# A routed mixture of experts behind attention: router folded into the weights, experts sorted by size

## The chip, the core and the metric

One core of a Trainium2 chip runs the whole program in one launch. The time is device microseconds from the first to the last instruction with what the launch adds around them, the median of several executions. Engines are named as in the profile: PE (TensorE products), PEld (its weight loads), DVE (VectorE), ACT (ScalarE), POOL (GpSimd), SP (SyncE, which here only issues DMAs).

## What is computed

Attention over 2 x 8 heads of 576 tokens, a gated feed-forward, and a mixture of eight experts in which every token goes to one expert and an expert takes at most 288 tokens.

```python
x = block_causal_attention(q, k, v)               # -> 1152 tokens x 512
x = (x @ w_a * (x @ w_b)) @ w_out                 # 512 -> 1536 -> 512, weights in float64
logits = x @ w_gate                               # 512 -> 8
expert = argmax(logits); gate = softmax(logits)[expert]
# token i is kept if fewer than 288 earlier tokens chose its expert
h = maximum(x @ w1[expert], 0)                    # 512 -> 1024
out[i] = gate * (h @ w2[expert])                  # 1024 -> 512; 0 where not kept
```

## The kernel before

Float32 accuracy is reached with pairs: a tensor is split into a first part in the fast product format (`fp32r`) and the rest in the same format, and a product takes three products of parts (first with first, first with second, second with first). ACT makes the first part with a cast, DVE or POOL the second with a subtraction. Where a plain float32 product is used (the logits), no split is needed.

**First feed-forward** (after the attention; lines 426 and 503 to 504). For each of twelve groups of 128 columns and each of three chunks of 384 tokens, `prod` (L426) forms two products of 12 steps each, and `gate_mul` multiplies them into `g_sb` (ACT copies one, DVE multiplies). The weights come as float64 words; `bits64` (L371 to L383) turns a tile into float32 with one ACT step and four DVE steps. Tiles called raw and bits have two buffers each, used in turn by the groups of `w_a`, `w_b` and by `w_out` (`load_wout`, `bits_wout`, `split_wout`), which is made ready in the same loop.

**Second product and router.** For each tile of 128 tokens t, `g_split` (L478, L479) splits g, `y_part` (L622) runs 12 x 3 products of 512 columns, `y_row` (L629) copies the result to a row buffer. Between the products of tile t stand the router's steps of tile t - 1: `y_turn` (L636) turns the row, `logits` (L644) multiplies it by `w_gate` in plain float32, `choose` (L651 to L665) finds the expert, `place` (L674 to L692) counts tokens with a triangular product, and POOL scatters the row into `xdisp`, a buffer in DRAM with 288 slots for each expert. All of that is in program order on each engine.

**Experts.** In the order of their numbers, two steps overlapped: the first product of expert e (`one`), then the second of expert e - 1 (`two`). Chunks of 1 MB of `w1` and `w2` are fetched by SP in a fixed order through five buffers (L573) and split by ACT (L591) and by DVE or POOL (L594), whatever the expert's size. `xload` (L775 to L779) reads the expert's rows, `x_turn` (L805, L813) turns them. An expert with over 64 tokens takes the wide way: products of 288 (or 256) columns at L841, then blocks of 128 tokens at L927 and a last block of 32 with both parts side by side (`stacked`, L823). One with 1 to 64 tokens has both parts of its 64 rows side by side in the stationary operand (L823), sums them (`both`, L973 and L974), turns the result (`turn_few`, L890) and multiplies again. Every choice is a branch (`tc.If`, L867 and others) on all engines, on a count read into registers. `put` (L909) scatters the result to `out` from POOL.

Of the kernel before, what the change touches and what calls it, by code (L numbers as in the profile page):

```python
# [27 lines left out]
NC_IDENT, NC_TRI, NC_IOTA, NC_TOK = 0, 128, 256, 264  # L28
# [29 lines left out]
def const_columns(n_tok, n_exp):  # L58
    """Identity, strict upper triangle, expert numbers, token numbers with two zeros after each."""
    import numpy as np  # L60

    nt = n_tok // P
    c = np.zeros((P, NC_TOK + 3 * nt), np.float32)
    c[:, NC_IDENT:NC_IDENT + P] = np.eye(P)
    c[:, NC_TRI:NC_TRI + P] = np.triu(np.ones((P, P)), 1)
    c[:, NC_IOTA:NC_IOTA + n_exp] = np.arange(n_exp)
    c[:, NC_TOK::3] = np.arange(P)[:, None] + P * np.arange(nt)[None, :]
    return c
# [3 lines left out]
def fused_kernel(ctx: ExitStack, tc, q, k, v, w_a, w_b, w_out, w_gate, w1, w2, consts, out, cap):  # L72
# [27 lines left out]
    ident = cst[:, NC_IDENT:NC_IDENT + P]  # L100
    xdisp = dpool.tile([NSLOT, ROW], F32, name="xdisp")
# [7 lines left out]
    # ------------------------------------------------------------ attention  # L109
# [8 lines left out]
    # rows of the dispatch buffer that no token fills: zeros, and a token number out of range  # L118
# [311 lines left out]
    def ahead(f, j):  # L430
        """Products of the first tokens, while the last heads are still turned."""
# [26 lines left out]
    # ------------------------------------------------ first feed-forward, a * b  # L458
# [5 lines left out]
    wg_sb = gp.tile([P, KD, E], F32, name="wg_sb")  # L464
    nc.sync.dma_start(out=wg_sb, in_=w_gate.rearrange("(k p) e -> p k e", p=P))
# [34 lines left out]

    def gate_mul(f, c, pa, pb):
# [9 lines left out]
    load_wout(0)  # L511
    es_y = ExitStack()
    psY = es_y.enter_context(tc.tile_pool(name="psY", bufs=2, space=PSUM))
    with tc.tile_pool(name="psF", bufs=3, space=PSUM) as psF:
        for f in range(NF):
            for c in range(NCH):
# [26 lines left out]
    es_r = ExitStack()  # L543
    wr_pool = es_r.enter_context(tc.tile_pool(name="wr_pool", bufs=5, side="right"))
    wq_pool = es_r.enter_context(tc.tile_pool(name="wq_pool", bufs=2, side="right"))
    HALF = 512
    NSL = 6
    CPE = F2 // HALF
    KC = KF2 // KD
    PER = CPE + KC  # L550
    chunks = [(0, 0, c) for c in range(CPE)]
    for e in range(E):
        if e + 1 < E:
            chunks += [(e + 1, 0, c) for c in range(CPE)]
        chunks += [(e, 1, c) for c in range(KC)]
    place_of = {x: n for n, x in enumerate(chunks)}
    wc = {}
    wpools = [wq_pool]
    state = {"raw": 0, "split": 0}
    raws = {}  # L560

    def fetch_chunk():
        n = state["raw"]
        if n >= len(chunks):
            return
        state["raw"] += 1
        e, which, c = chunks[n]
        raw = wr_pool.tile([P, KD, HALF], F32, tag="wraw", name=f"wraw{n}")
        if which == 0:
            src = w1[e, :, c * HALF:(c + 1) * HALF].rearrange("(k p) f -> p k f", p=P)  # L570
        else:
            src = w2[e, c * KD * P:(c + 1) * KD * P, :].rearrange("(k p) f -> p k f", p=P)
        nc.sync.dma_start(out=raw, in_=src)  # L573
        raws[n] = raw

    def split_next():
        """Pieces of the split of the next chunk into its two parts."""
        n = state["split"]
        if n >= len(chunks):
            return []  # L580
        state["split"] += 1
        while state["raw"] <= n:
            fetch_chunk()
        pool = wpools[0] if n % NSL < 2 else wpools[1]
        raw = raws.pop(n)
        hi = pool.tile([P, KD, HALF], F32R, tag="whi", name=f"whi{n}")
        lo = pool.tile([P, KD, HALF], F32R, tag="wlo", name=f"wlo{n}")
        wc[chunks[n]] = (hi, lo)

        def piece(a):  # L590
            nc.scalar.copy(hi[:, a:a + 2], raw[:, a:a + 2])  # L591
            e, which, c = chunks[n]
# [448 lines left out]
```

## Time and profile before

| | us |
|---|---|
| median of 3 runs (lowest, highest) | 554.28 (553.45, 555.82) |
| span of the profiled execution | 551.1 |
| PE busy, share of the span | 494.1, 90% |
| DVE | 333.3, 60% |
| ACT | 259.9, 47% |
| POOL | 212.8, 39% |
| mean granted clock of PE | 0.965 |

The profiled execution is one of its own; its span leaves out the launch. A busy PE is not PE at its peak, since products are pipelined: start to start is the pace, and the duration of one product is longer than its pace. Times in the trace are microseconds from the start of the span. The reader should look at stretches, not at the shares of the whole span: attention ends at about 140 us, the first feed-forward at 283.5, the second product at 378, and the experts fill the rest.

### The profile page before, as it was taken

How to read it: one execution, taken by the hardware profiler on the slowest of the kernel's cores; microseconds unless marked ns; L12 is line 12 of the kernel's file. 1: busy time of each engine (PE TensorE's matmuls, PEld its weight loads, DVE VectorE, ACT ScalarE, POOL GpSimd, SP SyncE). 2: the span in 40 equal slices, each digit the busy share in tenths (PEclk: the TensorE clock that was granted, in tenths of full speed). 3: DMA queues.
4: the chain of work that ended last, by engine and by line, in shares of the span. 5: the costliest groups of instructions: out<-in, count | busy, mean ns of one | idle time of the engine just before them, and what ended most of it. 6: DMA issues, size and time to landing. Idle time of an engine off the chain costs nothing. (4 is left out here: it accounts for less than half of the span.)

```text
span 551.1 us, 8356 instructions
## 1 busy us (share of the span) xinstructions
PE 494.1 (90%) x2860; PEld 437.7 (79%) x2860; DVE 333.3 (60%) x567; ACT 259.9 (47%) x502; POOL 212.8 (39%) x215
## 2 busy tenths in 40 slices
PE   5899989999999999999999999995397989897764
PEld 4799879999999999999997766773297888575553
DVE  4799899863565566763333445333578535257991
ACT  4798687863242343322222423211566545357740
POOL 6557584770041522313100301011324606184971
PEclk9899999999999999999999999998589999999887
DMA  6774575100544442421027122000479736475810
GB/s 149 204 242 124 124 230 177 29 2 1 180 143 140 150 153 78 152 81 74 1 94 288 40 96 96 19 24 2 157 251 296 262 141 201 162 259 179 271 52 4
DMA packets 67251, 73.39 MB, mean 133 GB/s; under 512 B 31394, under 2 KB 43810, under 8 KB 67184
## 3 DMA queue, kind: packets, MB, share of 16 engines
q1 hardware_dynamic: 65584, 69.09, 39.2%
q0 software_dynamic: 1456, 3.29, 1.6%
q8 instruction: 38, 0.62, 0.5%
q14 instruction: 29, 0.24, 0.1%
q10 hardware_dynamic: 144, 0.15, 0.1%
HBM read 62.12 MB, written 11.72 MB: 134 GB/s over the span
## 5 line engine op out<-in xcount | busy, mean ns | idle before, releaser
L426 PE MATMUL p<-xTh,hi 128*128 128x384 f32 x272 | 91.1, 335 | 1.6 <-ACT asb L503 0.8
L426 PE MATMUL p<-xTh,lo 128*128 128x384 f32 x272 | 90.9, 334 | 0.0
L426 PE MATMUL p<-xTl,hi 128*128 128x384 f32 x272 | 90.9, 334 | 0.0
L594 DVE TENSOR_TENSOR wlo<-wraw,whi 128x1024 fp32r<-128x1024 f32 x43 | 78.3, 1837 | 14.4 <-ACT whi L591 13.5
L594 POOL TENSOR_TENSOR wlo<-wraw,whi 128x1024 fp32r<-128x1024 f32 x21 | 57.4, 2747 | 44.9 <-ACT whi L591 29.4
L314 POOL TENSOR_TENSOR PB<-PB,rs 128x64 f32<-128x64 f32 (+8 forms) x72 | 54.0, 782 | 32.3 <-DVE rs L307 18.8
L591 ACT CAST whi<-wraw 128x1024 fp32r<-128x1024 f32 x64 | 63.9, 1047 | 4.5 <-issue 3.3
L426 PEld LDWEIGHTS p<-xTh,hi 128*128 128x128 f32 x272 | 51.0, 188 | 2.2 <-ACT asb L503 1.2
L389 POOL TENSOR_TENSOR wol<-wob,woh 128x1024 fp32r<-128x1024 f32 x6 | 14.4, 2401 | 96.9 <-ACT woh L388 96.9
L426 PEld LDWEIGHTS p<-xTl,hi 128*128 128x128 f32 x272 | 51.1, 188 | 0.0
L426 PEld LDWEIGHTS p<-xTh,lo 128*128 128x128 f32 x272 | 51.0, 188 | 0.0
L622 PE MATMUL py<-woh,gh 128*128 128x512 f32 x108 | 45.7, 423 | 0.0
L841 PE MATMUL ph<-xt,whi 128*128 128x288 f32 (+1 forms) x192 | 40.2, 307 | 5.8 <-ACTq L887 1.7
L692 POOL DMA_INDIRECT xdisp<-row,sl x9 | 9.0, 999 | 88.8 <-ACT row L629 83.9
L622 PE MATMUL py<-woh,gl 128*128 128x512 f32 x108 | 42.8, 396 | 0.0
L622 PE MATMUL py<-wol,gh 128*128 128x512 f32 x108 | 42.5, 394 | 0.0
L296 ACT ACTIVATE PB<-sc,nm 128x64 f32<-128x64 f32 (+8 forms) x72 | 37.7, 534 | 6.7 <-DVE nm L286 6.4
L330 DVE TENSOR_TENSOR PTl<-pT,PTh 128x512 fp32r<-128x512 f32 (+1 forms) x56 | 33.4, 623 | 8.2 <-ACT PTh L326 7.9
L841 PEld LDWEIGHTS ph<-xt,whi 128*128 128x128 f32 x192 | 32.0, 199 | 7.0 <-ACTq L887 2.1
L504 DVE TENSOR_TENSOR g_sb<-asb,p 128x384 f32<-128x384 f32 x34 | 18.4, 552 | 31.6 <-PE p L426 17.7
L416 POOL TENSOR_TENSOR lo<-bits,hi 128x1024 fp32r<-128x1024 f32 x12 | 28.8, 2396 | 20.2 <-ACT hi L410 20.2
L286 DVE TENSOR_REDUCE nm<-sc 128x1 f32<-128x64 f32 (+8 forms) x72 | 32.1, 478 | 6.8 <-PE sc L266 6.6
(147 smaller groups left out, 1153.4 us busy)
## 6 DMA issues: line engine op xcount, KB each, us to landing
wraw<-in_moe_w SPq DMA_DIRECT2D x32, 1024.0 KB, 6.4
raw<-in_moe_w_a SPq DMA_DIRECT2D x12, 512.0 KB, 3.6
raw<-in_moe_w_b SPq DMA_DIRECT2D x12, 512.0 KB, 4.7
wor<-in_moe_w_out SPq DMA_DIRECT2D x6, 1024.0 KB, 4.9
xdisp<-zrow SPq DMA_DIRECT2D x6, 774.0 KB, 5.4
out<-zrow SPq DMA_DIRECT2D x3, 768.0 KB, 4.8
qkv<-in_q SPq DMA_DIRECT2D x16, 128.0 KB, 2.5
qkv<-in_k SPq DMA_DIRECT2D x16, 128.0 KB, 2.8
```

The costliest lines, as they stand in the source:

```text
L286: nc.vector.tensor_reduce(out=soft[n][0][:, col[i]:col[i] + 1], in_=view, op=ALU.max, axis=ax, negate=True)
L296: nc.scalar.activation(out=dst, in_=view, func=AF.Exp, bias=nm[:, col[i]:col[i] + 1], accum_out=sm[:, col[i]:col[i] + 1],)
L314: nc.gpsimd.tensor_tensor(out=x, in0=x, in1=r, op=ALU.mult)
L330: nc.vector.tensor_tensor(out=PTl[:, sl], in0=src, in1=f32(PTh[:, sl]), op=ALU.subtract)
L389: nc.gpsimd.tensor_tensor(out=lo, in0=f32(m), in1=f32(hi), op=ALU.subtract)
L416: nc.gpsimd.tensor_tensor(out=lo, in0=f32(m), in1=f32(hi), op=ALU.subtract)
L426: nc.tensor.matmul(ps, lhsT=lt, rhs=rt, start=(n_ == 0), stop=(n_ == len(seq) - 1))
L504: nc.vector.tensor_tensor(out=g_sb[:, f, c * CH:(c + 1) * CH], in0=asb, in1=pb, op=ALU.mult)
L591: nc.scalar.copy(hi[:, a:a + 2], raw[:, a:a + 2])
L594: eng.tensor_tensor(out=lo[:, a:a + 2], in0=raw[:, a:a + 2], in1=f32(hi[:, a:a + 2]), op=ALU.subtract)
L622: nc.tensor.matmul(s["py"], lhsT=lt[:, f], rhs=rt[:, f], start=(f == 0 and i == 0), stop=(f == NF - 1 and i == 2))
L841: nc.tensor.matmul(ph[:, 0:n].rearrange("p (g c) -> p g c", c=G), lhsT=lt, rhs=rt, start=(n_ == 0), stop=(n_ == len(seq) - 1),)
```

## The change

- **Router ahead of the second product.** Since `logits = g @ w_out @ w_gate`, the product `w_out @ w_gate` is formed once. For that `w_out` comes a second time, transposed on the host (`in_w_outT`, 6 MB in float64), through the same raw and bits buffers. `gate_rows` multiplies a tile by `w_gate` padded to 32 columns in plain float32, the four row blocks to four groups of 32 PSUM partitions; `gate_cols` adds the four and turns them with one product against `sel`, a 0/1 matrix. The logits of all tokens are then formed from `g_sb` in one go (`logit_rows`), `choose` and `place` run once for all tiles, while the first tile of the second product runs. Each tile's row is scattered right after `y_row`.
- **Experts sorted.** `place` ranks the experts by count; slots in `xdisp` go by rank. Rank, expert's number and the number of experts with over 32 tokens are read into registers. SP fetches weights by a register's expert number, eight chunks already during the second product, into a ring of ten buffers.
- **One tree of branches.** `arms` picks one of nine straight programs, `experts(n)`, for n large experts. In it each large expert has 288 columns, blocks of 128 (the later ones only if its count asks for them) and a tail of 32; for the split all second parts are on DVE.
- **Small experts in float32.** Experts with at most 32 tokens go in groups of four, 32 rows each, unsplit. `few1` forms the four row blocks of a contraction in four groups of 32 PSUM partitions; `few_turn` adds and turns them with `sel`; `few2` does the second product likewise, `few_sum` adds its four groups into the expert's place, `group_out` scales and writes all four at once. `line` interleaves these steps of four experts by hand. Experts without tokens are not fetched.

```diff
+    def gate_rows(c):
+        m = wt_bits.pop(c)
+        pw = psW.tile([P, 2 * P], F32, tag="pw", name=f"pw{c}")
+        for kd in range(KD):
+            nc.tensor.matmul(pw[G * kd:G * (kd + 1)], lhsT=wgp[:, kd], rhs=f32(m)[:, kd], start=True, stop=True)
+        t = xpool.tile([P, 2 * P], F32, tag="wpT", name=f"wpT{c}", bufs=2)
+        nc.scalar.copy(t, pw)
+        wt_bits[c] = t
+    def gate_cols(c):
+        t = wt_bits.pop(c)
+        pf = psW.tile([P, 2, G], F32, tag="pf", name=f"pf{c}")
+        for i in range(2):
+            nc.tensor.matmul(pf[:, i], lhsT=t[:, i * P:(i + 1) * P], rhs=sel[:, 0:G], start=True, stop=True)
+        nc.scalar.copy(Wp[:, 2 * c:2 * c + 2], pf)
...
                 if c == 1 and f % 2 == 0:
+                    bits_wot(f // 2)
+                    load_wout(f // 2)
+                if c == 1 and f % 2:
                     bits_wout(f // 2)
                     if f // 2 + 1 < NWO:
-                        load_wout(f // 2 + 1)
+                        load_wot(f // 2 + 1)
                     split_wout(f // 2)
+                    gate_cols(f // 2)
+                if c == 0 and f % 2:
+                    gate_rows(f // 2)
...
+    def logit_rows(c):
+        pl = psG.tile([P, CH], F32, tag="pl", name=f"pl{c}", bufs=3)
+        for f in range(NF):
+            j = f % KD
+            nc.tensor.matmul(
+                pl[G * j:G * (j + 1)], lhsT=Wp[:, f], rhs=g_sb[:, f, c * CH:(c + 1) * CH],
+                start=(f < KD), stop=(f >= NF - KD), skip_group_check=True,
+            )
+        nc.scalar.copy(lgp[:, c], pl)
...
+    def choose():
+        for t in range(NT):
+            nc.tensor.matmul(plg[:, t], lhsT=flat[:, t * P:(t + 1) * P], rhs=sel[:, 0:E], start=True, stop=True)
...
+    def place():
+        nc.tensor.matmul(pp, lhsT=tri, rhs=oh, start=True, stop=False)
+        for t in range(NT):
+            nc.tensor.matmul(pp[:, t + 1:], lhsT=ones, rhs=bc(oh[:, t], 1, NT - t), start=False, stop=(t == NT - 1))
...
+    for c in range(NCH):
+        logit_rows(c)
     for t in range(NT):
-        y_part(t, 0, 2)
-        if t > 0:
-            y_turn(t - 1)
+        y_part(t, 0, 4)
+        if t == 0:
+            choose()
         if t + 1 < NT:
             g_split(t + 1)
-        if t > 0:
-            y_part(t, 2, 5)
-            logits(t - 1)
-            y_part(t, 5, 8)
-            choose(t - 1)
-            y_part(t, 8, 11)
-            place(t - 1)
-            y_part(t, 11, NF)
...
+        y_part(t, 4, NF)
         y_row(t)
-        if t in (2, 4):
-            split_to(t // 2)
-    y_turn(NT - 1)
-    logits(NT - 1)
-    choose(NT - 1)
-    place(NT - 1)
+        if t == 0:
+            place()
+            numbers_sp()
+            for r in range(2):
+                for c in range(NCK):
+                    raws[r, c] = ring[r * NCK + c]
+                    fetch(r, c)
+        if t == 5:
+            numbers()
+        scatter(t)
...
+    def few1(a, i):
+        hp = new("hp", [P, CPE, HALF], bufs=2, pool="few")
+        for c in range(CPE):
+            ph = psH.tile([P, HALF], F32, tag="ph", name=f"pf{a}_{i}_{c}_{uid[0]}")
+            for kd in range(KD):
+                nc.tensor.matmul(
+                    ph[kd * G:(kd + 1) * G], lhsT=g["xt"][:, kd, i * G:(i + 1) * G], rhs=raws[a + i, c][:, kd],
+                    start=True, stop=True,
+                )
+            (nc.vector.tensor_copy if c else nc.scalar.copy)(hp[:, c], ph)
+    def few_turn(a, i):
+        for f in range(KF2):
+            nc.tensor.matmul(pt[:, f], lhsT=hp[:, f * P:(f + 1) * P], rhs=sel[:, 0:G], start=True, stop=True)
+        g[i] = new("hg", [P, KF2, G], bufs=2, pool="few")
+        nc.scalar.activation(out=g[i], in_=pt, func=AF.Relu)
+    def few2(a, i):
+        for f in range(KF2):
+            j = f % KD
+            nc.tensor.matmul(
+                po[j * G:(j + 1) * G], lhsT=g[i][:, f], rhs=raws[a + i, CPE + f // KD][:, j],
+                start=(f < KD), stop=(f >= KF2 - KD), skip_group_check=True,
+            )
+        nc.vector.tensor_copy(out=g[i], in_=po)
+    def few_sum(a, i):
+        nc.tensor.matmul(
+            g["ps"][o:o + m], lhsT=sel[:, 0:m], rhs=g[i], start=True, stop=True, skip_group_check=True
+        )
+    def line(a):
+        for w in "00 01 10 02 20 11 03 21 12 30 22 13 31 23 32 33".split():
+            FEW[int(w[0])](a, int(w[1]))
+        group_out(a, 4)
...
+        for r in range(n):
+            if r + 1 < n:
+                x_turn(r + 1)
+                if r + 3 < n:
+                    xload(r + 3)
+                for piece in split_all(r + 1, one):
+                    piece()
+                used(r + 1, one)
+            elif groups:
+                es_h.close()
+                fs = pool(es_f, "fs", n, "right")
+                next_weights()
+                group_turn(*groups[0])
+            block(r, 0)
+            more(r, n)
+            if r + 1 < n:
+                first(r + 1, split_all(r + 1, two))
+                used(r + 1, two)
...
+    def arms(lo, hi, at):
+        if lo == hi:
+            return experts(lo)
+        with tc.If(nbig[0] > at) as over:
+            arms(at + 1, hi, (at + 1 + hi) // 2)
+        with over.Else():
+            arms(lo, at, (lo + at) // 2)
```

## Rows read from the trace of the kernel before

**Rows 1.** Busy time by stretch: length, then PE, PEld, DVE, ACT, POOL; clock, DMA.
```profile
140.80:283.50 142.70, 141.83 (x816) 141.46 (x817) 79.98 (x94) 46.73 (x65) 35.80 (x15) 1.00 0.33 110
283.50:378.00 94.50, 92.65 (x446) 68.64 (x444) 39.55 (x125) 24.52 (x45) 11.30 (x15) 1.00 0.26 96
378.00:398.50 20.50, 5.47 (x32) 3.84 (x32) 10.15 (x24) 7.75 (x14) 7.28 (x14) 0.61 0.28 87
398.50:495.00 96.50, 89.71 (x512) 76.74 (x512) 53.62 (x75) 51.89 (x77) 44.86 (x38) 0.98 0.67 227
495.00:545.10 50.10, 36.28 (x153) 27.38 (x152) 39.70 (x28) 28.57 (x36) 31.31 (x19) 0.86 0.42 142
545.10:551.10 6.00, 0.00 (x0) 0.00 (x0) 0.74 (x1) 0.68 (x1) 0.90 (x1) 0.89 0.03 6
```

**Rows 2.** Waits of PE, 385 to 552 us; groups by line, 410 to 552.
```profile
PE ptt L890 <- DVE hr L974: 4.8, 1, 4.8
...
L594 DVE TENSOR_TENSOR wlo<-wraw,whi 128x1024 fp32r<-128x1024 f32 x30 | 61.4, 2051 | 8.4 <-ACT whi L591 7.5 <-POOL gate L798 0.5 <-PE pf L823 0.4
```

**Rows 3.** Timeline of the second product (start, duration); L644 of the lines view.
```profile
283.55 0.39 PE L622 MATMUL py<-woh,gh 128*128 128x512 f32 x1
...
287.50 0.40 PE L622 MATMUL py<-woh,gl 128*128 128x512 f32 x1
...
292.11 0.59 ACT L629 COPY row<-py 128x512 f32<-128x512 f32 x1 [6.83 <-PE py L622]
...
295.62 0.40 PE L622 MATMUL py<-woh,gl 128*128 128x512 f32 x1
...
295.94 0.28 PE L644 MATMUL plt<-yT,wg_sb 128*8 128x128 f32 x1
...
295.94 1.04 PE L644 MATMUL plt<-yT,wg_sb 128*8 128x128 f32 x8
...
296.92 0.51 PE L622 MATMUL py<-woh,gh 128*128 128x512 f32 x1
...
302.62 0.59 ACT L629 COPY row<-py 128x512 f32<-128x512 f32 x1 [2.32 <-PE py L622]
...
L644 PE MATMUL plt<-yT,wg_sb 128*8 128x128 f32 x72 | 9.4, 273 | 2.4 <-DVE yT L638 2.4
```

**Rows 4.** Timeline of PE in a large expert's first product and a turn.
```profile
424.07 0.44 PE L841 MATMUL ph<-xt,whi 128*128 128x288 f32 x2
...
427.73 0.44 PE L841 MATMUL ph<-xt,whi 128*128 128x288 f32 x2
...
430.18 1.40 PE L805 MATMUL px<-cst,xd 128*128 128x128 f32 x12
```

**Rows 5.** Timeline of DVE in the feed-forward: one tile of `w_out`.
```profile
149.52 0.69 DVE L373 TENSOR_SCALAR wob<-wob 128x1024 f32<-128x1024 f32 x1
...
152.23 1.23 DVE L383 SCALAR_TENSOR_TENSOR wob<-wor,wob 128x1024 int32<-128x1024 int32 x1
```

**Rows 6.** Busy time in 402 to 442 us; timeline of the gap.
```profile
402.00:442.00 40.00, 37.06 (x247) 34.02 (x247) 26.36 (x42) 24.59 (x39) 20.26 (x21) 0.99 0.80 268
...
377.96 0.58 ACT L629 COPY row<-py 128x512 f32<-128x512 f32 x1 [2.39 <-PE py L622]
...
385.18 0.98 POOL L692 DMA_INDIRECT xdisp<-row,sl  x1 [4.91 <-DVE cnt L727]
385.92 3.88 ACT L591 CAST whi<-wraw 128x1024 fp32r<-128x1024 f32 x4 [3.30 <-issue]
386.99 2.36 DVE L594 TENSOR_TENSOR wlo<-wraw,whi 128x1024 fp32r<-128x1024 f32 x2 [2.38 <-ACT whi L591]
387.51 1.44 SPq L775 DMA_DIRECT2D xd<-xdisp  x2
...
394.74 2.53 PE L805 MATMUL px<-cst,xd 128*128 128x128 f32 x12 [4.04 <-PEq L867]
...
398.57 0.77 PE L841 MATMUL ph<-xt,whi 128*128 128x256 f32 x2 [1.30 <-ACT whi L591]
```

More of the change, by code (lines that the diff above doesn't have):

```diff
@@ L556, in fused_kernel @@
[L556 to L592, printed above, removed]
-            eng = nc.gpsimd if e and ((which, a) == (1, 2) or (which, c, a) == (0, 1, 0)) else nc.vector
-            eng.tensor_tensor(out=lo[:, a:a + 2], in0=raw[:, a:a + 2], in1=f32(hi[:, a:a + 2]), op=ALU.subtract)
-        return [partial(piece, a) for a in range(0, KD, 2)]
@@ L932, in blocks @@
-    def blocks(e, j, todo):
-        s = st[e]
-        r, m = blks[j]
-        po = block(e, j)
-        for piece in todo[:2]:
-            piece()
-        if TAIL and j == len(blks) - 1:
-            gated(e, j, m, po)
-        else:
-            nc.scalar.activation(out=s["y"][j][:m], in_=po[:m], func=AF.Copy, scale=s["gate"][j][:m, 0:1])
-        put(e, j, m)
-        todo = todo[2:]
-        if j + 1 < len(blks):
-            with most(e, blks[j + 1][0]) as more:
-                blocks(e, j + 1, todo)
-            if todo:
-                with more.Else():
-                    for piece in todo:
-                        piece()
-        else:
-            for piece in todo:
-                piece()
@@ L956, in two @@
-    def two(e, todo):
-        s = st[e]
-        s["y"] = [mp.tile([P, DM], F32, tag="y", name=f"y{e}_{j}", bufs=3) for j in range(len(blks))]
-        with most(e, HB) as big:
-            blocks(e, 0, todo)
-        with big.Else():
-            with least(e):
-                po = psO.tile([P, DM], F32, tag="po", name=f"pq{e}")
-                stacked(po, HB, [s["ht"][:, f, 0:P] for f in range(KF2)], w2_rows(e))
-                gated(e, 0, HB, po)
-                put(e, 0, HB)
-            for piece in todo:
-                piece()
@@ new lines, in fused_kernel, with new, xload @@
+    full = cap // P
+    TAIL = cap - full * P
+    assert 0 < TAIL <= G
+    REST = full * P
+    st, parts = {}, {}
+    uid = [0]
+    mp = {}
+    def new(tag, shape, dt=F32, bufs=1, pool="all"):
+        uid[0] += 1
+        return mp[pool].tile(shape, dt, tag=tag, name=f"{tag}_{uid[0]}", bufs=bufs)
+    def xload(r):
+        s = st[r] = {}
+        s["xd"] = new("xd", [P, full, ROW], bufs=2, pool="big")
+        s["xe"] = new("xe", [TAIL, ROW], bufs=2, pool="big")
+        for j in range(full):
+            nc.sync.dma_start(out=s["xd"][:, j], in_=xdisp[r * cap + j * P:r * cap + (j + 1) * P, :])
+        nc.sync.dma_start(out=s["xe"], in_=xdisp[r * cap + REST:(r + 1) * cap, :])
@@ new lines, in more, with group_load, group_turn @@
+    def more(r, n, j=1):
+        with tc.If(many[r] > j * P):
+            if j < full:
+                block(r, j)
+                more(r, n, j + 1)
+            else:
+                tail_block(r)
+    def group_load(a, n):
+        g = st["g", a] = {}
+        g["xd"] = new("xg", [P, ROW])
+        for i in range(n):
+            nc.sync.dma_start(out=g["xd"][i * G:(i + 1) * G], in_=xdisp[(a + i) * cap:(a + i) * cap + G, :])
+    def group_turn(a, n):
+        g = st["g", a]
+        m = n * G
+        pt = psT.tile([P, KD, P], F32, tag="pt", name=f"pg{a}_{uid[0]}")
+        for kd in range(KD):
+            nc.tensor.transpose(pt[:, kd, :m], g["xd"][:m, kd * P:(kd + 1) * P], ident[:m, :m])
+        g["xt"] = new("xgt", [P, KD, P])
+        nc.vector.tensor_copy(out=g["xt"][:, :, :m], in_=pt[:, :, :m])
+        g["ti"] = new("tg", [P, 1], I32)
+        nc.gpsimd.tensor_copy(out=g["ti"][:m], in_=g["xd"][:m, DM + 1:DM + 2])
@@ new lines, in fused_kernel, with single, pool @@
+    FEW = (few1, few_turn, few2, few_sum)
+    def line(a):
+        for w in "00 01 10 02 20 11 03 21 12 30 22 13 31 23 32 33".split():
+            FEW[int(w[0])](a, int(w[1]))
+        group_out(a, 4)
+    def single(a, i, n):
+        for step in FEW:
+            step(a, i)
+        if i + 1 < n:
+            with tc.If(many[a + i + 1] > 0):
+                single(a, i + 1, n)
+    def pool(es, name, n, side=None):
+        return es.enter_context(tc.tile_pool(name=f"{name}{n}", bufs=1, **({"side": side} if side else {})))
```

633 lines of the change are left out of this document (336 added, 297 removed).

## The prediction

> **What bounds the kernel now.** I read the busy time by stretch first, because shares over the whole span mix stages with different limits. The stretches of [rows 1] are cut where the trace passes from one kind of TensorE work to the next: the first feed-forward, the second product with its router, the gap between the last row of the second product and the experts' first product, the experts while large ones are in work, the small experts, and the tail. In the feed-forward PE is busy 141.8 of 142.7 us and in the second product 92.7 of 94.5, both at full clock, while no other engine passes 56%. There PE alone sets the end: what PE gets or loses there goes into the span one for one. In the gap of 20.5 us PE works 5.5 us and its clock is 0.61. With large experts PE works 89.7 of 96.5 us. With the small ones it works 36.3 of 50.1 us, with DVE at 39.7, POOL at 31.3 and ACT at 28.6: the splitting of weights into two parts is what PE waits for. The longest wait of PE there, 4.8 us in one piece [rows 2], is for DVE's sum hr, and DVE comes to it late because it has the parts of the next weights ahead of it in its queue. The chain that ended last names the rows written to `out`, but those are POOL's writes waiting for one another beside PE's work; I don't use it. The span is 551.1 us, the median 554.3; the 3.2 us around it I leave alone and put every change on 554.3.
>
> **What the inputs make of it.** The reference's routing, worked out on its inputs, gives counts of 640 (cut to 288), 274, 217, 14, 3, 2, 2 and 0. So the new tree takes the arm for three large experts; four have at most 32 tokens and take the float32 way in one group; the empty one is skipped, its 4 MB too. The trace of before agrees: three experts in wide products, four in stacked ones.
>
> **Two prices first.** A single-part product (two-part operands, three such products) of 512 columns comes every 0.2324 us: 17 starts between 283.55 and 287.50 in [rows 3]. A plain float32 product appears as two records, each with a weight load of its own (72 records for 9 x 4 products [rows 3]). One record of 128 columns lasts 0.28 us and eight together last 1.04 [rows 3], so records follow at 0.76 / 7 = 0.109 us, and one float32 product costs 2 x 0.109 / 128 = 1.70 ns a column. A change from one kind to the other and back costs about 0.2 us: 295.62 to 296.92 is 1.30, less 0.23 for the product before and 8 x 0.109 [rows 3].
>
> **The new column-tiled products.** Three new places use float32 products with 32 stationary columns, written to four different groups of 32 partitions in turn: gate_rows (24 of 256 columns), logit_rows (36 of 384) and few1 with few2 (64 of 512). One after another they cost (6,144 + 13,824 + 32,768) x 1.70 ns = 10.5 + 23.5 + 55.7 = 89.7 us. What they cost in truth depends on how many of them run in the array at once, and no row of before has two products in different column groups. The bounds: all in line, 89.7 us; all four groups at once, 22.4. I take two at once. The records in [rows 3] go in program order, load, product, load, product. The two records of one product use the same 32 columns, so the second can't start before the first is through; the next product's first record, in other columns, can go beside it. Then each product costs one record's time, 44.9 us, and each burst leaves one record over at its end (6 of 0.22, one of 0.33, 8 of 0.44: 5.1), together 50.0 us.
>
> The 8-column products of [rows 3] already leave most columns idle and still pay the whole price, but they all stand at the same place, so they say nothing on that. The Trainium skill speaks for overlap: its page "TensorE: Matmul & The Clock Gate", section "Part 3: Packing small matmuls — row/col tiling", gives 2.38 times for three column tiles and 3.07 times for four row tiles, and says that products start and end in program order. By 3.07 the sum would be 89.7 / 3.07 = 29.2 in place of 50.0. No run here shows either.
>
> **First feed-forward.** PE gets the 24 products above. gate_cols adds 12 float32 products with 128 stationary columns and 32 moving ones, 24 records; the nearest row is twelve small transposes in 1.40 us [rows 4], 0.117 each: 2.8 us. Twelve visits of another kind cost 12 x 0.2 = 2.4. ACT and DVE turn six more tiles from float64; DVE's four steps take 3.94 us each [rows 5], 24 us on 80 of 142.7 busy [rows 1], with three banks for each product between PE and them. I book 1 us for stalls, between 0 and 8 if a load of 1 MB comes late (the two raw buffers now turn four times in two column groups, not three). SP's six more loads stand ahead of nothing that is due sooner. Fixed part: +6.2.
>
> **Second product.** Two copies of finished rows stand 10.51 us apart [rows 3]; 36 products take 36 x 0.2324 = 8.37. So turning the rows, the logits, choosing and placing cost 2.14 us for each of eight tiles that have them between products, and 17.1 go. New beside logit_rows: choose with 18 records at 0.117 (2.1), place with 10 tiny bfloat16 products (at most 1.2, as transposes), three switches (0.6) and up to 1 us in which the first logits wait for PSUM that the last multiplication still reads (0.5). Their chains on DVE lie beside y_part's products. The register loads ahead of tile 6 are short beside PE's queue; 0 to 2 us, I take nothing. SP fetches eight chunks of 1 MB in this stretch: at the 268 GB/s of [rows 6] 31 us, beside 85 us of products. Fixed part: 4.4 - 17.1 = -12.7.
>
> **The gap.** Now the last tile still turns, finds its logits, is chosen and placed: from the row copy at 377.96 to its scatter at 385.18 are 7.2 us [rows 6]. After the change only the copy, 0.6, and a small POOL copy stand ahead of the scatter, so it starts some 6 us sooner. Behind it nothing changes in kind: 2.3 us to the issue of the load, some 3 for landing, turning and casting. What is late next is DVE. Four parts at 1.18 each (two in 2.36 [rows 6]) now stand ahead of the turned rows' second parts, and ACT needs 3.9 us for its four casts, after a branch that took 3.3 [rows 6]: 0.9 + 3.3 + 3.9, then about 1.2 for the last part, 1.7 for three second parts and 0.8 for hand-overs, about 12. So 20.6 becomes 12: -8.6, between -4 (the tree's jumps cost another 4, as the wait of 4.04 for a branch in [rows 6]) and -11 (jumps hidden).
>
> **The experts.** From 398.5 to 545.1 are 146.6 us. After: 27 products from 424.07 to 427.73 give 0.1356 us for 288 columns [rows 4]; 3 x 96 of them are 39.1. Six blocks of 24 at 0.2324 are 33.5, two tails of 16 are 7.4, two turns at 1.40 [rows 4] are 2.8. The cold start costs 1.9 (a mean clock of 0.98 over 96.5 us [rows 1]) as it does now. PE's other idle time here is now 96.5 - 89.7 = 6.8; block(r) no longer stands behind a turn, so I keep 4. Sum 88.7. Nothing but the large experts is split, 8 pieces each; DVE's take 2.05 us as long as POOL splits beside it [rows 2], and 1.18 without [rows 6]. DVE then needs 9.4 us for an expert's parts, in 26 to 29 us of products: hidden, at 2.05 still 16.4. The small ones: 64 records of few_turn at 0.117 (7.5), four sums of 512 columns (3.5), 16 switches (3.2), 2 for the drain: 16.2, plus the 64 tiled products. ACT, DVE and SP issue less than that: two casts, a relu and a copy for each expert, and 1 MB takes 3.9 us, 8 MB 31 us, which begin during the last large expert. 146.6 goes to 104.9, -41.7, plus few1 and few2. Last cast, scale and write of 6.0 us [rows 1] stay.
>
> **Sum.** Fixed: 6.2 - 12.7 - 8.6 - 41.7 = -56.8. Tiled products, two at once: +50.0. Together -6.8: 554.3 - 6.8 = **547.5 us**.
>
> **The rivals.** *In line.* If a product in another column group waits until the one before is through, the tiled products cost 89.7: +32.9, 587 us, slower. The place is the feed-forward (about +17 against before), the logits and the small experts (72 us in place of the 50.1 of [rows 1]). It decides from the point at which a product costs over 56.8 / 89.7 = 63% of its lone price. For it speaks that every record of before that follows another does so after a whole stream; against it only that the places differ. *All four.* If each group goes on by itself, 22.4 to 29.9 us (four, or three in effect): -34 to -27, 520 to 527, middle 522. This is what the packing rule of the Trainium skill's TensorE page points to; by the order of the two records I hold it for less likely than two. *Cover gone.* Two at once, but the jumps of the tree, loads behind freed buffers, or late bits in the feed-forward take 8 to 14 us more (their bounds: 4 + 2 + 7, and 4 for one far jump among the small experts): 556 to 561. That the change doesn't do what it says would need more than 32 tokens in a small expert, which the counts exclude.
>
> **How the numbers follow.** Two at once 0.47; all four 0.30; in line 0.15; cover gone 0.08. The likeliest alone reaches from 538 to 557. About 0.5% is what a measurement of this kernel can tell from no change, here 551.5 to 557. From two at once I count 0.32 as faster, 0.11 as same, 0.04 as slower; all four is faster, the other two slower: 0.62, 0.11, 0.27. The range leaves out being in line and little else: 515 to 572.
>
> **What would show it.** Start-to-start of few1's records at 512 columns: 0.44 us in pairs for two at once, about 0.87 for each product alone in line, four within 0.9 for all four. The second product's stretch should take 94.5 us less 0.6 (two at once: 11.8 + 0.3 - 12.7), the gap 12, the large experts 89, the small ones from the last large block to the last product 48, the feed-forward 155. If the small experts show PE idle behind a DMA, the fetch order was the step that failed; if the gap stays near 20, the branches were.

## The result and the profile after

| | before | after |
|---|---|---|
| median (lowest, highest), us | 555.05 (553.45, 555.83) | 531.05 (529.34, 532.41) |
| span of the profiled execution | 551.1 | 528.4 |

The ratio is 0.9548, with a 95% interval from 0.9505 to 0.9591: 24 us less, where 6.8 less was forecast. The direction held and the time lies in the range, but the size is over three times the one given; the rival called "all four" (520 to 527) is nearer than the forecast of 547.5.

The first view is busy time by stretch for the kernel after, cut at the same changes of work as [rows 1]: length, then PE, PEld, DVE, ACT and POOL busy with their counts, granted clock (a share of full speed), DMA share, GB/s. In order: feed-forward, second product, gap, large experts, small experts, tail; the last line is a part of the feed-forward.

```profile
141.30:298.70 157.40, 150.88 (x888) 146.30 (x888) 104.00 (x118) 56.02 (x80) 35.05 (x14) 0.98 0.42 140
298.70:383.80 85.10, 82.98 (x425) 65.26 (x424) 20.16 (x41) 19.04 (x23) 19.44 (x19) 1.00 0.33 119
383.80:394.50 10.70, 2.96 (x14) 1.94 (x13) 5.86 (x7) 5.91 (x8) 2.95 (x8) 0.75 0.53 148
394.50:481.70 87.20, 84.66 (x492) 74.47 (x492) 40.83 (x78) 36.41 (x57) 9.84 (x18) 0.97 0.62 214
481.70:517.10 35.40, 29.80 (x201) 14.40 (x200) 5.54 (x8) 4.47 (x9) 0.97 (x1) 0.86 0.35 130
517.10:528.40 11.30, 0.61 (x5) 0.50 (x4) 0.29 (x1) 0.69 (x1) 1.16 (x2) 0.57 0.07 21
...
156.44:160.37 3.93, 3.93 (x17) 3.12 (x18) 3.83 (x5) 0.61 (x2) 0.00 (x0) 0.50 0.73 243
```

Against [rows 1], stretch by stretch, with what the prediction's own terms give. The column "at the measured price" keeps every fixed term and puts what the tiled float32 products took (below) in the place of "two at once".

| stretch | before | forecast | at the measured price | after | after minus that |
|---|---|---|---|---|---|
| feed-forward | 142.7 | 155.5 | 152.3 | 157.4 | +5.1 |
| second product | 94.5 | 93.9 | 87.7 | 85.1 | -2.6 |
| gap | 20.5 | 12.0 | 12.0 | 10.7 | -1.3 |
| large experts | 96.5 | 88.7 | 88.7 | 87.2 | -1.5 |
| small experts | 50.1 | 47.6 | 30.1 | 35.4 | +5.3 |
| tail | 6.0 | 6.0 | 6.0 | 11.3 | +5.3 |

So two things went otherwise. The tiled products came far cheaper than booked (about 27 us), and three places took nearly 16 us that the sum did not have.

**The tiled products.** PE's timeline of the kernel after: start, duration of the group, instruction, and in brackets the idle time before it with what ended it. The first two lines are the logits and the product behind them; the next two are the same logits cut off at 301.0 and at 303.0; the two behind these are a turn of `gate_rows` and the product behind it; the last two are one `few1` and the `few2` behind it.

```profile
300.97 6.01 PE L609 MATMUL pl<-g_sb,Wp 128*32 128x384 f32 x72 [2.12 <-DVE g_sb L544]
306.91 0.50 PE L722 MATMUL py<-woh,gh 128*128 128x512 f32 x1
...
300.97 0.53 PE L609 MATMUL pl<-g_sb,Wp 128*32 128x384 f32 x4 [2.12 <-DVE g_sb L544]
...
300.97 2.46 PE L609 MATMUL pl<-g_sb,Wp 128*32 128x384 f32 x28 [2.12 <-DVE g_sb L544]
...
184.39 0.64 PE L529 MATMUL pw<-wtb,wgp 128*32 128x256 f32 x8
184.96 0.45 PE L430 MATMUL p<-xTh,hi 128*128 128x384 f32 x1
...
502.31 1.92 PE L937 MATMUL pf<-fs,xgt 128*32 128x512 f32 x16
504.05 1.90 PE L959 MATMUL pq<-rawB,hg 128*32 128x512 f32 x16
```

From start to the start of what follows: 5.94 us for 36 logits products, where 36 x 2 x 384 columns in line were priced at 23.5; 0.57 for four products of `gate_rows`; 1.74 for eight products of `few1`, or 0.87 for four, within the 0.9 that the prediction names for all four groups. Four records start together, and four more every 0.325 us (4 by 301.0, 28 by 303.0). At full clock that is 5.94 + 6 x 0.57 + 8 x 1.74 = 23.3 us in total, against 50.0 booked and 89.7 in line.

**The three places.** PE's waits in the kernel after (line, what it waited for, total, times, longest; three of them), then the timeline of each place.

```profile
PE pw L529 <- issue: 6.5, 1, 6.5
...
PE pf L937 <- ACT hp L941: 4.7, 1, 4.7
...
PE pg L924 <- DMA xg<-xdisp: 3.3, 1, 3.3
```

```profile
151.21 2.78 POOL L420 TENSOR_TENSOR lo<-bits,hi 128x1024 fp32r<-128x1024 f32 x1 [12.50 <-ACT hi L414]
151.83 3.24 DVE L383 SCALAR_TENSOR_TENSOR wtb<-wtr,wtb 128x1024 int32<-128x1024 int32 x1
155.11 1.23 DVE L387 SCALAR_TENSOR_TENSOR wtb<-wtr,wtb 128x1024 int32<-128x1024 int32 x1
156.44 1.08 PE L529 MATMUL pw<-wtb,wgp 128*32 128x256 f32 x8 [6.52 <-issue]
...
482.46 2.85 PE L937 MATMUL pf<-rawA,xgt 128*32 128x512 f32 x24 [0.65 <-PEq L905]
484.47 0.97 POOL L863 DMA_INDIRECT out<-y,ti  x1 [6.11 <-DMA out<-y,ti]
489.42 1.07 ACT L941 COPY hp<-pf 128x512 f32<-128x512 f32 x2 [6.88 <-DMA out<-y,ti]
489.49 0.69 DVE L941 COPY hp<-pf 128x512 f32<-128x512 f32 x1 [17.18 <-DMA out<-y,ti]
490.06 1.94 PE L937 MATMUL pf<-rawA,xgt 128*32 128x512 f32 x8 [4.75 <-ACT hp L941]
491.92 3.62 PE L950 MATMUL ph_t<-cst,hp 128*128 128x32 f32 x16
...
516.06 1.05 PE L972 MATMUL ps<-q,cst 128*32 128x512 f32 x2 [0.20 <-DVE q L964]
520.44 0.60 PE L924 MATMUL pg<-cst,xg 32*128 32x32 f32 x4 [3.33 <-DMA xg<-xdisp]
522.31 0.18 POOL L928 CAST tg<-xg 32x1 int32<-32x1 f32 x1 [2.72 <-DMA out<-y,tg]
```

In the feed-forward PE stands at the first `gate_rows` until 0.1 us after DVE has finished the last bits of its tile (155.11 + 1.23 = 156.34). DVE's step before that took 3.24 us, where the same step (L383) takes 1.23 on the later tiles; POOL's subtraction L420 ran beside it until 153.99, and the step ended 1.1 us behind that. When PE goes on, the granted clock is 0.50 (the lower level, 1.2 GHz) until 160.37, as the part of the feed-forward above shows; 3.93 us of products at half speed cost some 2 us more, an estimate. At the start of the small experts, ACT and DVE can't write `hp`, the copy of the first products, until the last large expert's scatter has landed: both name `out<-y,ti`. PE fills its PSUM buffers with 24 records, then waits 4.75 us. In the tail a second group of small experts is loaded and turned, after the last sum, though only the empty expert would be in it.

**The gap.** ACT, POOL, DVE and PE in the kernel after; it answers to the timeline in [rows 6].

```profile
384.14 0.59 ACT L729 COPY row<-py 128x512 f32<-128x512 f32 x1 [7.66 <-PE py L722]
385.48 0.98 POOL L734 DMA_INDIRECT xdisp<-row,sl_i  x1 [7.07 <-ACT row L729]
386.99 3.88 ACT L835 CAST hi<-rawA 128x1024 fp32r<-128x1024 f32 x4 [2.26 <-issue]
388.22 4.63 DVE L836 TENSOR_TENSOR lo<-rawA,hi 128x1024 fp32r<-128x1024 f32 x4 [16.94 <-ACT hi L835]
390.41 2.16 PE L816 MATMUL px<-cst,xd 128*128 128x128 f32 x8 [6.44 <-DMA xd<-xdisp]
392.77 1.28 DVE L819 TENSOR_TENSOR xt<-px,xt 128x512 fp32r<-128x512 f32 x2
```

From the row copy to its scatter are 1.34 us, where [rows 6] had 7.22. The rows are turned from 390.41 on, but DVE starts on their second parts only at 392.77, as soon as it has done four parts of weights.

### The profile page after: what moved, and what is told of

The parts are those of the page before. It is cut to its first block, busy times and chain, and to the rows that moved or that the text cites. A ratio compares the mean times of both kernels' runs of the same rounds, so it can differ in the third digit from the quotient of the medians.

```text
span 528.4 us, 7937 instructions
## 1 busy us (share of the span) xinstructions
PE 479.6 (91%) x2924; PEld 422.1 (80%) x2924; DVE 286.3 (54%) x471; ACT 222.1 (42%) x445; POOL 150.9 (29%) x174
## 5 line engine op out<-in xcount | busy, mean ns | idle before, releaser
L430 PE MATMUL p<-xTh,hi 128*128 128x384 f32 x272 | 92.8, 341 | 0.7 <-DVE g_sb L544 0.7
L420 POOL TENSOR_TENSOR lo<-bits,hi 128x1024 fp32r<-128x1024 f32 x12 | 30.4, 2531 | 43.2 <-ACT hi L414 43.2
L722 PE MATMUL py<-woh,gh 128*128 128x512 f32 x108 | 42.6, 394 | 0.0
L851 PE MATMUL ph<-xt,hi 128*128 128x288 f32 x192 | 40.2, 305 | 0.4 <-ACT xt L818 0.4
L334 DVE TENSOR_TENSOR PTl<-pT,PTh 128x512 fp32r<-128x512 f32 (+1 forms) x56 | 33.5, 624 | 8.1 <-ACT PTh L330 7.8
L486 DVE TENSOR_TENSOR gl<-g_sb,gh 128x1536 fp32r<-128x1536 f32 x9 | 15.8, 1755 | 38.9 <-ACT gh L485 38.9
L836 DVE TENSOR_TENSOR lo<-rawA,hi 128x1024 fp32r<-128x1024 f32 x20 | 24.0, 1224 | 22.8 <-ACT hi L835 22.8
L330 ACT CAST PTh<-pT 128x512 fp32r<-128x512 f32 (+1 forms) x56 | 28.7, 545 | 15.2 <-PE pT L325 14.6
L543 ACT COPY asb<-p 128x384 f32<-128x384 f32 x34 | 16.4, 482 | 43.6 <-PE p L430 43.6
L347 PE MATMUL px<-PTh,VZh 128*128 128x320 f32 (+4 forms) x112 | 33.8, 302 | 0.3 <-DVE xTl L366 0.3
```

The source lines that it names most:

```text
L330: nc.scalar.copy(PTh[:, sl], src)
L334: nc.vector.tensor_tensor(out=PTl[:, sl], in0=src, in1=f32(PTh[:, sl]), op=ALU.subtract)
L347: nc.tensor.matmul(px[:, o_:o_ + cnt * BLK], lhsT=lt, rhs=rt[:, t0:t0 + cnt, h * BLK:(h + 1) * BLK], start=(kt == 0 and h == 0 and n_ == 0 ...
L420: nc.gpsimd.tensor_tensor(out=lo, in0=f32(m), in1=f32(hi), op=ALU.subtract)
L430: nc.tensor.matmul(ps, lhsT=lt, rhs=rt, start=(n_ == 0), stop=(n_ == len(seq) - 1))
L722: nc.tensor.matmul(s["py"], lhsT=lt[:, f], rhs=rt[:, f], start=(f == 0 and i == 0), stop=(f == NF - 1 and i == 2))
```

## The experiments

Theories at the start: **A**, PE starts products in program order, each as soon as its own 32 columns are free; **B**, PE looks past a product that waits, and each column group goes on by itself. The prediction's "two at once" would give 11.7 us for the logits in any order, and the 5.94 of the kernel after had already ruled it out. Each ratio is against the kernel before, run in the same session: 556.67 us for the two orders of the logits, the router alone and the transposed weights; 556.25 for the marks, the tail and all three; 555.65 for all in one group and the columns later.

**One group after the other.** In each of the three chunks of tokens (`logit_rows` runs once for each) the three logits products of one column group stand in a row.

```diff
-        for f in range(NF):
+        for f in sorted(range(NF), key=lambda f: f % KD):
```

> The changed kernel with only the order of the 36 logit products altered: all products of one group of 32 columns in a row (f = 0, 4, 8, 1, 5, 9, ...) in place of 0, 1, 2, 3, .... Work and result are the same. In the changed kernel the 36 products take 5.9 us (300.97 to 306.91), four records starting together every 0.325 us. Theory A (a product starts when its turn in program order has come and its own 32 columns are free; other groups don't hold it): in a run of three of one group the next group's first starts with the third, so 24 steps of 0.65 us and one more, 16.3 us; total +10.4, 541.5 us. Rival B (PE looks past a waiting product into the other groups): about 6 us, no change, 531. Rival C (products never overlap and a product with 32 columns is just cheap): 5.9 us, no change, 531; B and C are told apart by whether four records start together. Rival D (overlap only where four groups follow one another strictly, else in line): 23.5 us, 548.5.

534.3 us, ratio 0.9592 [0.9576, 0.9608].

**Two groups in turn.** As above, but in each chunk six products alternate between two groups, then six between the other two.

```diff
-        for f in range(NF):
+        for f in sorted(range(NF), key=lambda f: f % KD // 2):
```

> As the run before, but the order alternates between two groups for six products, then between the other two (f = 0, 1, 4, 5, 8, 9, 2, 3, ...). Theory A: pairs start together every 0.65 us and the third pair shares its time with the next two groups' first pair: 4 steps of 0.65 for each chunk of 12 products and one more at the end, 8.5 us, total +2.6, 533.6 us. What the prediction took for the original order (two at once whatever the order): 11.7 us, total +5.8, 537. Look-ahead (rival B): 6 us, 531.

530.4 us, ratio 0.9539 [0.9517, 0.9561]. PE's timeline of the first experiment (two lines), its busy time in two parts of the logits, and PE's timeline of the second (two lines):

```profile
301.37 11.15 PE L609 MATMUL pl<-g_sb,Wp 128*32 128x384 f32 x72 [2.12 <-DVE g_sb L544]
312.44 0.50 PE L722 MATMUL py<-woh,gh 128*128 128x512 f32 x1
...
301.37:304.74 3.37, 3.37 (x12) 1.08 (x14) 0.06 (x1) 0.00 (x0) 1.49 (x2) 0.50 0.00 0
304.74:312.44 7.70, 7.70 (x66) 3.14 (x60) 0.00 (x0) 0.96 (x2) 0.00 (x0) 1.00 0.01 2
```

```profile
300.82 6.68 PE L609 MATMUL pl<-g_sb,Wp 128*32 128x384 f32 x72 [2.12 <-DVE g_sb L544]
307.43 0.50 PE L722 MATMUL py<-woh,gh 128*128 128x512 f32 x1
```

The logits take 11.07 us group by group and 6.61 in pairs, beside 5.94 in rotation. But group by group the granted clock was 0.50 (the lower level, 1.2 GHz) for the first 3.37 us, and 1.00 throughout for the other two. What that costs is seen in the experiment "Marks kept" (below), which has the logits in rotation, with the clock as low for 3.41 us:

```profile
301.92 7.71 PE L609 MATMUL pl<-g_sb,Wp 128*32 128x384 f32 x72 [2.12 <-DVE g_sb L544]
309.56 0.50 PE L722 MATMUL py<-woh,gh 128*128 128x512 f32 x1
...
302.14:305.55 3.41, 3.41 (x24) 1.08 (x20) 0.06 (x1) 0.00 (x0) 1.29 (x2) 0.50 0.00 0
```

There rotation takes 7.64 us, 1.70 more than at full clock. So the order by groups costs about 3.4 us (11.07 against 7.64), and would take some 9.4 at full clock, an estimate.

Theory A gives more for both than was measured (16.3 and 8.5 us), theory B less for the first (6). If products started strictly in program order, the first of a group could not start before the third of the group ahead, two lone products of 0.65 us later: 24 such steps in three chunks, 15.6 us up to the last start, and 12 steps or 7.8 us for the pairs. Both were faster, the first even at a lower clock. So, as far as the compiled program keeps the order of the kernel's text, which no run checks, PE passes over a product that waits for its columns and starts a later one in free columns; but it reaches only a limited way ahead. How far was not measured.

**All in one group.** The disputed price by itself: every logits product goes to the first 32 partitions, and `choose` contracts 32 rows.

```diff
-                pl[G * j:G * (j + 1)], lhsT=Wp[:, f], rhs=g_sb[:, f, c * CH:(c + 1) * CH],
-                start=(f < KD), stop=(f >= NF - KD), skip_group_check=True,
+                pl[0:G], lhsT=Wp[:, f], rhs=g_sb[:, f, c * CH:(c + 1) * CH], start=(f == 0), stop=(f == NF - 1),
```

> The changed kernel with all 36 logit products written to one group of 32 partitions, summed there, in place of four groups in turn; the sum over groups falls away with it. This is the lone price of such a product. If the price by records holds (0.32 us for a record of 384 columns, two records, nothing overlapping in one group) the logits take 36 x 0.65 = 23.4 us in place of 5.9, total +17.5 or a little more where the clock falls, 547 to 549 us. Rival: products with 32 columns are cheap by themselves, or PE overlaps them even in one group; then clearly less, 531 to 538.

548.0 us, ratio 0.9882 [0.9797, 0.9966]. PE's timeline of this experiment:

```profile
302.81 23.41 PE L608 MATMUL pl<-g_sb,Wp 128*32 128x384 f32 x72 [2.12 <-DVE g_sb L544]
326.14 0.50 PE L720 MATMUL py<-woh,gh 128*128 128x512 f32 x1
```

The logits take 23.33 us at full clock, 17.4 more than in rotation, and the kernel takes some 17 more than the one after (548.0 against 531.05, with runs from 545.79 to 552.21). The lone price of the prediction, 23.5, is right; only the overlap was not.

**Router alone.** The kernel before with the first part of the change (rows of `w_out` times `w_gate`, `logit_rows`, `choose` and `place` for all tiles at once, `scatter` after each row) and the old experts. Its logits lie in a buffer of the second `g_split` tile.

```diff
+    for c in range(NCH):
+        logit_rows(c)
...
-        y_part(t, 0, 2)
-        if t > 0:
-            y_turn(t - 1)
+        y_part(t, 0, 4)
```

> The kernel before with the router's part of the change alone (w_out times w_gate in the feed-forward, logits of all tokens at once, one choice and placing, scatter behind each row); the experts stay as before: slots by expert number, split weights for every size, the old branches. To fit, the logits lie in a buffer that the second tile's split uses later, and rows have two buffers, not three. If the three stretches ahead of the experts carry over as in the changed kernel (feed-forward +14.7, second product -9.3 us) and the gap shrinks by what scatter no longer waits for (-6 to -9), the total is -1 to -4 against before: 551 to 554 us, and the experts' part of the change is worth about 20. Rival: the gap shrinks only because sorted experts begin with fetched and ready weights; then the gap stays near 20 and the total is +4 to +6, 559 to 561.

560.88 us, ratio 1.0071 [1.0046, 1.0096]. Busy time by stretch of this experiment, feed-forward, second product, gap, all experts:

```profile
140.90:299.50 158.60, 151.61 (x888) 146.97 (x888) 104.28 (x119) 56.00 (x80) 35.04 (x14) 0.98 0.42 139
299.50:386.50 87.00, 84.89 (x425) 65.61 (x424) 22.91 (x35) 22.72 (x27) 20.05 (x19) 0.98 0.29 104
386.50:403.10 16.60, 3.33 (x17) 2.57 (x17) 8.26 (x9) 8.41 (x12) 6.13 (x12) 0.62 0.50 157
403.10:555.10 152.00, 130.15 (x664) 107.63 (x664) 89.28 (x103) 79.19 (x111) 77.16 (x57) 0.90 0.56 185
```

With the router alone the kernel is slower than before, by 0.7%. The feed-forward pays 15.9 us, the second product gives back 7.5 and the gap 3.9, so the three cost 4.5 us together. The total is that of the rival, though the gap did shrink, only by less than the first theory needs. The whole gain of the change comes with the experts: 0.9548 against 1.0071, some 29 us. The gap gave 3.9 here and 9.8 in the full change, which suggests that the rest needs the new fetches and tree of branches too; no run took these alone. The old experts took 152.0 us in place of 146.6 [rows 1], at a granted clock of 0.90 where [rows 1] has 0.98 and 0.86; the lower clock goes with the longer time, but what came first stays open.

**The transposed weights first.** The first tile of transposed `w_out` is fetched ahead of the fourth column group of `w_a` and `w_b`, and turned from float64 earlier.

```diff
-    load_wab(3)
     load_wot(0)
+    load_wab(3)
...
+                if (f, c) == (0, 0):
+                    bits_wot(0)
...
-                    bits_wot(f // 2)
+                    if f:
+                        bits_wot(f // 2)
```

> The changed kernel with the first tile of the transposed w_out loaded and turned to float32 ahead of the fourth column group's, not behind it. In the changed kernel PE stands 6.5 us at 156.4, ahead of the first gate_rows, because DVE finishes that tile only at 156.3. Theory: nothing else is late there, the wait goes, feed-forward about 151 in place of 157.4 us, total -5 to -6.5, 525 us. Rival: the fourth column group's weights are now late by as much and PE waits for them at its fourth group; total 531.

529.24 us, ratio 0.9523 [0.9494, 0.9551]: not to be told from the kernel after. PE's waits in this experiment:

```profile
PE pf L538 <- ACT wpT L531: 3.5, 1, 3.5
```

The wait of 6.5 us at the first `gate_rows` is gone, but PE now waits 3.5 one step later, at the first `gate_cols`, for ACT's copy, and 1.1 at the second `gate_rows`. The stall moved; the stretch lost 1.5 us.

**Marks kept.** Theory: the small experts' wait comes from the buffers of the large experts. Token numbers and gates (`ti`, `te`, `gate`) lie in the pool "big", whose space the small experts use again, and `ti` is read by the scatter until it lands. The experiment gives these three a pool that isn't used again.

```diff
-        s["ti"], s["gate"] = (new(x, [P, full], y, 2, "big") for x, y in (("ti", I32), ("gate", F32)))
-        s["te"], s["ge"] = new("te", [TAIL, 1], I32, 2, "big"), new("ge", [P, 2], F32, 2, "big")
+        s["ti"], s["gate"] = (new(x, [P, full], y, 2) for x, y in (("ti", I32), ("gate", F32)))
+        s["te"], s["ge"] = new("te", [TAIL, 1], I32, 2), new("ge", [P, 2], F32, 2, "big")
```

> The changed kernel with the token numbers and gates of the large experts (ti, gate, te, ge) in the pool that lives through all experts, not in the one that the small experts' buffers take over. In the changed kernel ACT and DVE start the first small expert's copies hp only at 489.4 us, when the write of the last large block to out has landed (issued 484.5), and PE stands 4.75 us and then runs part of the next products at the lower clock. Theory: hp lies where that write still reads its token numbers; with them elsewhere the wait goes: PE's idle 4.75 us and about 1.5 to 2 us of low clock, total -5 to -7, 525 us. Rival: the write's row buffer or the branch behind the last block holds ACT, and the wait stays: 531.

522.75 us, ratio 0.94 [0.9353, 0.9448]. The small experts' stretch and the first lines of PE's timeline there:

```profile
484.00:510.40 26.40, 25.55 (x201) 12.33 (x200) 5.54 (x8) 4.57 (x9) 0.97 (x1) 1.00 0.46 175
...
484.69 3.64 PE L937 MATMUL pf<-rawA,xgt 128*32 128x512 f32 x32 [0.65 <-PEq L905]
488.26 1.97 PE L950 MATMUL ph_t<-cst,hp 128*128 128x32 f32 x16
```

The stretch falls from 35.4 to 26.4 us. The wait of 4.75 is gone and all 32 records of `few1` run through. The data rows `y`, which the scatter reads too, lie in a pool that isn't used again, before and after the edit; which of the three moved tiles counts was not separated, but the trace names `ti`. The other 4 us are the clock: 1.00 granted where it was 0.86, and the 16 turning records behind the wait take 1.97 us, not 3.62.

**Tail inside the branch.** The second group of small experts is loaded and turned only if it has tokens.

```diff
-            if i:
+            if i and m == 4:
                 group_load(a, m); group_turn(a, m)
...
+                if i:
+                    with tc.If(many_sp[a] > 0):
+                        group_load(a, m)
                 with tc.If(many[a] > 0):
+                    if i:
+                        group_turn(a, m)
                     single(a, 0, m)
```

> The changed kernel with the second group's (the empty expert's) row load and turn put inside branches on its count, so that they don't run here. In the changed kernel 11.3 us pass from the last product's end (517.1) to the end of the span, in the kernel before 6.2. Theory: POOL's cast of the empty group's token numbers waits for the last write to land, because it reuses that buffer, and the branches and the end come after it; without it -3 to -5, 526 to 528 us. Rival: the end waits for the jump out of the tree whatever stands before it; then the tail stays near 11 and the total at 531.

528.71 us, ratio 0.9514 [0.946, 0.9567]: not separable by the time. In the trace the tail falls from 11.3 to 8.8 us; the fetch and the turn are gone. The 2.8 us that remain against the tail of 6.0 [rows 1] stay open.

**All three.** The last three edits together.

> The changed kernel with the three edits of the runs on the first tile, the marks and the empty group together. If the three waits are independent their gains add: -13 to -18, 513 to 518 us. If one only uncovers another (the small experts then wait for weights: ft and fs are issued at the same time as hp today), less: 520 to 524.

518.39 us, ratio 0.9332 [0.9285, 0.9379], the fastest kernel here. Small experts and tail in the view of stretches:

```profile
480.30:507.10 26.80, 25.94 (x202) 12.33 (x200) 5.53 (x8) 4.56 (x9) 0.97 (x1) 1.00 0.47 176
507.10:515.60 8.50, 0.00 (x0) 0.00 (x0) 0.00 (x0) 0.69 (x1) 0.98 (x1) 0.71 0.08 18
```

The gains add, as far as the noise tells: 0.9548 - 0.9332 is 12.0 us of 556, and the three alone gave by their ratios 1.4, 8.2 and 1.9, of which only the 8.2 stands clear of it.

**Columns later.** On top of these, the first `gate_cols` one chunk later, at f = 1 and c = 2.

```diff
-                    gate_cols(f // 2)
+                    if f > 1:
+                        gate_cols(f // 2)
+                if (f, c) == (1, 2):
+                    gate_cols(0)
```

> The three edits together and the first gate_cols one chunk of 384 tokens later. In the run with the first tile ahead, PE's wait of 6.5 us ahead of the first gate_rows became one of 3.5 us ahead of the first gate_cols, because ACT's copy wpT stands behind the first step of the next column group's weights, which wait for their load. Theory: one chunk later (4.2 us of products) that copy is done; -3 against the three edits, 515 us. Rival: the products behind it wait for ACT's copies instead; 518.

521.39 us, ratio 0.9397 [0.9337, 0.9457]: no gain. PE's longest wait in the feed-forward is now at the second `gate_rows`:

```profile
PE pw L529 <- DVE wtb L387: 6.1, 1, 6.1
```

Without the earlier stall PE comes there at 178.0 us, 6 us sooner than in the kernel after, and DVE ends the tile at 183.9. Its step L383 took 3.24 us again, begun (179.43) while POOL's L420 ran (178.81 to 181.59). So part of the wait, 2.0 of 6.1 us here as of the 6.5 above, goes with this meeting of POOL and DVE; no run took the two apart. Three orders of the same steps have given waits of 6.5, 3.5 and 6.1 us at three places. What has to change to remove this stall, and not move it, stays open.

## Why the prediction was wrong

**The step that failed is "two at once".** The prediction read, from records that come as load, product, load, product, that PE works through single records in program order, and that the second record of a product must wait for the first while only one neighbour fills in. The order in which the trace lists products at one place was taken for a rule between places. In the kernel after the first records of four products start together (4 records by 301.0), each ahead of the second record of the first product, and four groups go on beside each other: 23.33 us in one group, 5.94 in four, 3.93 times less. The term was 50.0 us, and the runs show 23.3.

The Trainium skill's page "TensorE: Matmul & The Clock Gate", section "Part 3: Packing small matmuls — row/col tiling", which the prediction weighed and put second, pointed the right way: groups overlap. Its factors, 2.38 for three column tiles and 3.07 for four row tiles, are smaller than the 3.93 measured here for four column groups of plain float32. Its statement that products start and end in program order doesn't agree with the 11.07 us of the first experiment, where strict order needs at least 15.6, if the compiled program keeps the order of the text.

**What the sum lacked.** With the measured 23.3 the fixed terms, -56.8, would have given 554.3 - 33.5 = 520.8 us. The kernel took 10 more.
- *Stalls in the feed-forward*, booked at 1 us between 0 and 8: one wait of 6.5, and some 2 us for the products at clock 0.50 behind it, just over the bound. The prediction looked for late loads and took DVE's 24 us for hidden. PE's wait ends with DVE's last step on the tile; 2.0 us of it are the step that ran 3.24 us beside POOL's subtraction, in place of 1.23. The stretch is 5.1 over its terms, so the others came in some 2 us lower; no run separates them.
- *The entry of the small experts*, not foreseen at all: 9.0 us from 35.4 to 26.4, shown by undoing it. The prediction looked for weights that land late and for jumps. It never asked who still reads the space that the small experts write. Without that wait the stretch is 26.4, below the 30.1 that the terms give.
- *The tail*, booked as unchanged: +5.3, of which 2.5 are shown to be the second group's fetch and turn. That the steps of a group without tokens stand outside the branch could be read in the code.

**What held.** The lone price of a float32 product (23.5 against 23.33 for the logits). The large experts (88.7 against 87.2), DVE's part of a split at 1.18 us without POOL beside it:

```profile
L836 DVE TENSOR_TENSOR lo<-rawA,hi 128x1024 fp32r<-128x1024 f32 x20 | 24.0, 1224 | 22.8 <-ACT hi L835 22.8
```

that is 1.22 (the line of the kernel after in the costliest groups, with busy time and mean ns), where [rows 2] had 2.05. The gap (12 against 10.7) for the reason given: the scatter comes 6 us sooner, and DVE, with four parts of weights ahead of the rows' second parts, is late next. ACT began its casts after a wait of 2.26, not the 3.30 of [rows 6]. The second product came 2.6 us below its terms; no run separates the causes.

**The rivals.** "All four" had the mechanism, and its 520 to 527 missed by the stalls; "cover gone" was right on late bits in the feed-forward, but stood on the wrong price; "in line" fell with the 23.33 against 5.94.

## What to carry to other kernels

Small-output products in plain float32 should be spread over all four groups of 32 columns, in rotation; the price was then about a quarter of the lone one (5.94 us against 23.33), and an order by groups gave away some 3.4 us of it (11.07 against 7.64 with the clock low for as long). When a stage with other buffers follows, list for each space that it reuses who reads it last: a scatter still in flight held up the whole next stage here, because small tiles of token numbers and gates lay in a reused pool. Code for cases that don't occur belongs inside the branch that tests for them, its loads too; here it took 2.5 us off the tail in the trace.

## What the hardware showed that was not expected

- Four groups of 32 columns run side by side in float32 at almost the whole factor: 36 products in 5.94 us against 23.33 in one group.
- PE doesn't hold to the order of the text among them: 11.07 us for groups one after the other, 6.61 for pairs, both below what starting in order allows (24 x 0.65 = 15.6, and 12 x 0.65 = 7.8). Yet with the clock low for as long, rotation took 7.64, so PE looks only some way ahead.
- The wait ahead of the logits is 2.1 us in every run that has them, and behind it the granted clock fell to 0.50 in four of the ten, for 3.4 us each: three with rotation took 7.64 us for the logits where those at full clock took 5.94. A comparison of two runs by one stretch needs the clock of both.
- A DVE step on a tile of `w_out` took 3.24 us in place of 1.23 where it began while POOL's subtraction ran, and ended 1.1 us behind that, in the kernel after and in the last experiment.
- A wait of 4.75 us cost 9.0: after it the granted clock of the stretch was 0.86 in place of 1.00, and the same 16 records took 3.62 us in place of 1.97.
